# Ups and downs in groups of three or four, with attention scores ahead of ups and attention outputs ahead of downs

## The chip, the cores and the metric

The kernel runs on one core of one Trainium2 chip. The metric is the device time of one execution in microseconds (us); lower is better. The engines of the core work side by side, each through its own list of instructions in order: TensorE (PE: matmuls, PEld: its weight loads), VectorE (DVE), ScalarE (ACT), GpSimd (POOL) and SyncE (SP, which issues most DMAs here). They wait for one another through semaphores.

## The reference

Eight batches of 576 tokens go through eight attention heads, four with a local mask and four with a strided one; the 4608 rows of 512 numbers that come out go through a feed-forward layer with a squared ReLU. All of it is float32.

```python
scores = scale * np.matmul(q, k.transpose(0, 1, 3, 2))
mask_local = (rel >= 0) & (rel < stride)                       # heads 0 to 3
mask_strided = (rel >= 0) & (pos[None, :] % stride == pos[:, None] % stride)  # heads 4 to 7
attn = np.exp(scores - max); attn = attn / (sum + 1e-09)
attn_out = np.matmul(attn, v)
x = attn_out.transpose(0, 2, 1, 3).reshape(4608, 512)
h = np.maximum(x @ w_in, 0.0)                                  # 512 -> 2048
out = h * h @ w_out                                            # 2048 -> 512
```

## The kernel before

**Tiles.** The 4608 rows are 12 chunks (`NCHUNK`) of 384 rows (`TC`). The 2048 columns of `h` are 16 slots (`NFT`) of 128. For each chunk `c` and slot `j` there are two pieces of TensorE work:

- an **up** (`up(c, j)`): 12 matmuls of 128x384 into one of three PSUM banks `h`. Each product is made of three, since every float32 is split in a high part and a low part (`xlh`, `xll` for local heads, `xsh`, `xsl` for strided ones). Then ScalarE does the ReLU (L487), the square (L488) and the rounded copy `gh` (L489), and VectorE the rest `gl = h - gh` (L490).
- a **down** (`down(c, j)`): 9 matmuls of 128x512 (L509), for each of three row tiles `y` the products `gh*w_hi`, `gh*w_lo`, `gl*w_hi` in that order. After slot 15 the three `y` are copied out of PSUM (L513) and written by DMA from SP (L514).

**Attention beside it.** While chunk `c` goes through its ups and downs, the attention of chunk `c + 1` is computed. Its four local heads (`pe_head`, chunks 2 to 11; chunks 0 and 1 go another way) are generators whose steps are drawn by `take`: DMA in; split of q and k (`kx`, `qx`: ACT and POOL); **scores** (4 matmuls, L237) with mask and row minimum on DVE (L241, L229); exponentials on ACT (L246), reciprocal of the sums on DVE (L247, L248) and multiplication by it on ACT (L251; for head 3 on POOL, L254); transposes of the result on DVE (L262) and its split (`px`: L270, L271, L272); **outputs** (4 matmuls, L283), put together by ACT (L286) and DVE (L287, L288) and split into `xlh`, `xll`. The strided heads run without TensorE: POOL multiplies (L426, L448), DVE sums up (L427, L449), in short pieces that `strided` yields and the loop draws at a given pace, for every slot a share.

**Order.** In chunk 0 each slot's up is followed by the down of two slots earlier. From chunk 1 on, slots go in pairs: up, up, then the downs of the two slots before. So a down comes at least two pairs of TensorE work after its up. `gpool` has two buffers for `gh` and two for `gl`: the `gh` of a slot waits for the down of two slots earlier. The table `plan` says between which of these blocks the heads' steps are drawn; scores and outputs stand now ahead of ups, now ahead of downs. `tc.issue_after` pins the order on TensorE. On the other engines the order in which the instructions of all these parts stand comes from the builder's scheduler; it is fixed when the program is built.

Of the kernel before, what the change touches and what calls it, by code (L numbers as in the profile page):

```python
# [18 lines left out]
STR = 32  # L19
# [26 lines left out]
WRATE = 2  # L46

# [39 lines left out]
def attn_moe(ctx: ExitStack, tc, qk_l, v_l, qk_d, v_d, qk_p, v_p, f_s, q_s, k_s, v_s, w_in, w_out, masks, eye, out):  # L87
# [4 lines left out]
    xpool = pool("xpool", 2)  # L92
    gpool = pool("gpool", 2)
    ypool = pool("ypool", 3)
# [4 lines left out]
    ps_y = pool("ps_y", NTT, space=PSUM)  # L99
    ps = pool("ps", 1, space=PSUM)  # L100

    def psum(i, nm):
# [96 lines left out]
    def pe_head(c, h):  # L199
# [60 lines left out]
        for r in range(QC // STR):  # L260
            for k in (r, r + 1):
                nc.vector.transpose(  # L262
                    out=pt[STR * k : STR * (k + 1), :, STR * r : STR * (r + 1)],
                    in_=e.rearrange("p (w k) -> p w k", k=KW)[STR * r : STR * (r + 1), :, STR * k : STR * (k + 1)],
                )
        src = pt.rearrange("p w q -> p (w q)")
        px = lpool.tile([P, 2, TC], F32R, name=f"px{u}", tag="px")

# [26 lines left out]
    def pe_pair(c, pr, local, qk, vr, es, pt, banks, sm, single):  # L295
# [67 lines left out]
        yield  # L363
        p4 = pt.rearrange("p (h w q) -> p h w q", h=2, w=NW)
        for h in range(2):
            t = s_ps[h] if s_ps else banks()

            for w in [*range(NW)] * (2 if c == 0 and local and not pr and h else 1):
                nc.tensor.transpose(t[:kw, w * QC : (w + 1) * QC], e4[h][:, w], ident[:QC, :QC])  # L369
            if c == 0 and not local:  # L370
                nc.vector.tensor_copy(pt[:kw, h * TC : (h + 1) * TC], t[:kw, :TC])
            else:
                last["a"] = nc.scalar.copy(pt[:kw, h * TC : (h + 1) * TC], t[:kw, :TC])
        yield
        x = x_tiles(c)
        if local:
            o = s_ps[0] if s_ps else banks()

            for w in [*range(NW)] * (3 if c == 0 and not pr else 1):
                for h in range(2):  # L380
                    nc.tensor.matmul(o[D * h : D * (h + 1), w * QC : (w + 1) * QC], v4[:kw, h, w], p4[:kw, h, w], start=True, stop=True)  # L381
            outs = [(o[:, :TC], [x["l", s][:, pr, :] for s in "hl"])]
        else:
# [3 lines left out]
            for a in range(2):  # L387
                o = s_ps[a]
                for w in range(NW):
                    for h in range(2):  # L390
                        p0 = r0 + STR * h
                        nc.tensor.matmul(o[p0 : p0 + STR, w * QC : (w + 1) * QC], v4[:kw, h, w, STR * a : STR * (a + 1)], p4[:kw, h, w], start=True, stop=True)
                by_i = lambda t: t[r0 : r0 + D].rearrange("p (s i r) -> p s i r", s=2, r=STR)
# [72 lines left out]
    def up(c, j):  # L466
# [4 lines left out]
        for kt in range(4):  # L471
# [3 lines left out]
            for w, xx in ((wi[p][0], xh), (wi[p][0], xl), (wi[p][1], xh)):  # L475
                done = nc.tensor.matmul(ph[:, :TC], w[:, wsl], xx, start=n == 0, stop=n == 11)  # L476
# [16 lines left out]

    def down(c, j):
        gh, gl = g_tiles.pop((c, j))
        p, o = divmod(j, 2)
# [8 lines left out]
        wsl = slice(o * DM, (o + 1) * DM)  # L505
        for t in range(NTT):
            sl = slice(t * P, (t + 1) * P)
            for k, (g, w) in enumerate(((gh, wo[p][0]), (gh, wo[p][1]), (gl, wo[p][0]))):
                done = nc.tensor.matmul(y_ps[c][t], g[:, sl], w[:, wsl], start=j == 0 and k == 0, stop=j == NFT - 1 and k == 2)  # L509
        if j == NFT - 1:  # L510
            for t in range(NTT):
                y = ypool.tile([P, DM], F32, name=f"ysb{c}_{t}", tag="ysb")
                (nc.scalar.copy if t == 1 else nc.vector.tensor_copy)(y, y_ps[c][t])  # L513
                nc.sync.dma_start(out=out[c * TC + t * P : c * TC + (t + 1) * P, :], in_=y)  # L514
        return done
# [17 lines left out]


    def pair_at(c, pr, local, place, psum_at):
        u = f"{c}_{pr}_{int(local)}"
        buf = lambda pl, nm, n, tag, **kw: pl.tile([P, n], F32, name=f"{nm}{u}", tag=tag, **kw)
        ee = lambda pl, tag: [buf(pl, f"e{h}", 512, tag) for h in range(2)]
        if place == 0:
            b = buf(lraw, "qk", TC + KC, "qk"), buf(lpool, "v", 512, "vx", bufs=1), ee(lpool, "e"), buf(lpool, "pt", 2 * TC, "px")  # L540
        elif place == 1:
            b = buf(lraw, "qk", TC + KC, "qk"), buf(ypool, "v", 512, "ysb"), ee(ypool, "ysb"), buf(lpool, "pt", 2 * TC, "px")
        elif place == 2:
            e = buf(xpool, "e", 2 * TC, "xlh")
            b = buf(xpool, "qk", 2 * TC, "xll"), buf(xpool, "v", 2 * TC, "xsl")[:, :512], [e[:, :TC], e[:, TC:]], buf(lpool, "pt", 2 * KC, "kx", bufs=1)[:, : 2 * TC]
        else:

            t = buf(wpool, "w", 2048, "w7")
            b = buf(xpool, "qk", 2 * TC, "xsh"), buf(spool, "v", 512, "s3", bufs=5), [t[:, :512], t[:, 512:1024]], t[:, 1024 : 1024 + 2 * TC]
        it = iter(range(10))  # L550
# [9 lines left out]
    def local(c):  # L560
# [7 lines left out]
    heads = {}  # L568
    plan = {
        0: ("", "0", "01"),  # L570
        1: ("", "1", "012"),
        2: ("", "0", "123"),
        3: ("", "1", ""),
        4: ("2", "", "23"),
        5: ("3", "", "23"),
        6: ("2", "", "3"),
        7: ("3", "", ""),
    }
# [74 lines left out]

    NS = NCHUNK * NFT
    for s in range(NS + 2):
        c, j = divmod(s, NFT)
        if s < NFT:

            with ExitStack() as seq:
                if s:  # L660
                    seq.enter_context(tc.issue_after(last["up"].ins))
                last["up"] = up(c, j)
            if s >= 2:
                last["pe"] = down(*divmod(s - 2, NFT))

        elif s % 2 == 0:
            before, between, rest = plan[j // 2]
            for part, slots, two in (up, (s, s + 1), before), (down, (s - 2, s - 1), between):
                take(c + 1, two)
                with tc.issue_after(last["pe"].ins):  # L670
                    for i in slots:
                        if 0 <= i < NS:
                            last["mm"] = part(*divmod(i, NFT))
                last["pe"] = last["mm"]
            take(c + 1, rest)
        if s < NFT - 2:

            weights = behind({"a": last["gh"]} | ({"x": last["xs"]} if s > NFT - 4 else {}), ungated)
            for _ in range(WRATE):
                next(weights, "end")  # L680
            weights_end = {e: last[e] for e in "agsv"}
        if s == LATER:
            zbank = (4,)
        if s == NFT - 1:
            with tc.issue_after(weights_end["g"].ins):
                for t in p_t:
                    nc.gpsimd.memset(t, 0.0)
        if j == NFT - 2:
            take(c + 2, "010")
        if c + 1 < NCHUNK and s >= LATER:  # L690
            j0 = LATER if c == 0 else 0
# [16 lines left out]
            if j == NFT - 1:  # L708
                run(lo)
                run(st)  # L710


# [74 lines left out]
```

## Time and profile before

| | |
|---|---|
| device time, median of 3 runs | 880.53 us (880.1 to 881.49) |
| the profiled execution, first to last instruction (span) | 877.8 us, 2.7 us under that median; its own whole time is not listed |
| chunk 6, from its first up to that of chunk 7 (452.14 to 522.21 us) | 70.07 us |
| TensorE busy in the span | 99% |
| VectorE, ScalarE, GpSimd busy | 73%, 65%, 77% |
| granted TensorE clock, mean of the span | 0.999 |

A busy TensorE is not one at its peak: matmuls overlap, and a record's length (334 to 392 ns) is longer than the step from one matmul to the next. The view by time gives the steps. The view of waits names, for each engine, what ended the idle time ahead of an instruction; idle time of an engine that nobody waits for costs nothing.

### The profile page before, as it was taken

What the parts mean: (1) busy time and instruction counts of PE and PEld (TensorE: products, weight loads), DVE (VectorE), ACT (ScalarE), POOL (GpSimd) and SP (SyncE); (2) the same over time, 40 slices, a digit from 0 to 9 for tenths busy, and PEclk for the clock granted to TensorE, in tenths of its full rate; (3) what the DMA queues carried; (4) which work ended last, traced back from release to release, by engine and by line L of the source; (5) the groups of instructions that cost most, each with busy time, mean ns of one, the idle gap of its engine ahead of it and who ended that gap; (6) DMA issues with size and microseconds to landing.
All of it is one profiled execution on the core that took longest, in us unless ns stands there. A gap on an engine that the chain in (4) does not pass through costs nothing.

```text
span 877.8 us, 14934 instructions
## 1 busy us (share of the span) xinstructions
PE 867.9 (99%) x4787; PEld 788.9 (90%) x4787; DVE 640.3 (73%) x1900; ACT 571.4 (65%) x1506; POOL 672.2 (77%) x718
## 2 busy tenths in 40 slices
PE   8999999999999999999999999999999999999997
PEld 7788899999999999999989898989898989999996
DVE  5796587797787887878878779878778787883111
ACT  6998776586576666657756758657666665664332
POOL 3689778877978989888988978996998899782000
PEclk9999999999999999999999999999999999999999
DMA  9963531223123023112102302312031021000000
GB/s 351 363 212 95 178 95 46 85 84 114 32 86 103 27 89 103 44 62 87 58 9 80 116 13 77 100 32 75 31 103 58 29 71 62 7 0 15 23 1 37
DMA packets 26799, 71.42 MB, mean 81 GB/s; under 512 B 2976, under 2 KB 8736, under 8 KB 25184
## 3 DMA queue, kind: packets, MB, share of 16 engines
q1 hardware_dynamic: 26432, 70.14, 24.1%
q8 instruction: 38, 0.62, 0.3%
q14 instruction: 41, 0.34, 0.1%
q10 hardware_dynamic: 288, 0.33, 0.1%
HBM read 61.01 MB, written 9.44 MB: 80 GB/s over the span
## 4 chain that ended last, share of the span: by engine, by line
PE 95%; ACT 2%; POOL 1%; issue 0%; DVE 0%; DVEq 0%; POOLq 0%; ACTq 0%
PE h L476 45%; PE y L509 45%; PE s L237 2%; PE o L283 2%; ACT b L353 1%; PE w_ps L606 1%; PE b L325 1%; POOL w L173 1%; ACT raw L154 0%; ACT z L166 0%; POOL pq L426 0%; ACT w L172 0%; PE b L381 0%; ACT xsh L396 0%; PE b L369 0%
## 5 line engine op out<-in xcount | busy, mean ns | idle before, releaser
L509 PE MATMUL y<-w,gh 128*128 128x512 f32 x1152 | 357.9, 391 | 0.5 <-POOL w L173 0.5
L509 PEld LDWEIGHTS y<-w,gh 128*128 128x128 f32 x1152 | 212.7, 188 | 40.5 <-POOL w L173 0.8
L476 PE MATMUL h<-xlh,w 128*128 128x384 f32 x768 | 229.1, 339 | 1.3 <-ACT xlh L396 0.6
L448 POOL TENSOR_TENSOR pp<-vs,sc 128x448 f32<-128x448 f32 (+10 forms) x192 | 190.0, 1014 | 48.8 <-DVE qs L449 23.0
L476 PE MATMUL h<-xsh,w 128*128 128x384 f32 x768 | 226.4, 335 | 0.3 <-POOL w L173 0.3
L509 PE MATMUL y<-w,gl 128*128 128x512 f32 x576 | 225.2, 392 | 0.0
L426 POOL TENSOR_TENSOR pq<-ks,qs 128x512 f32<-128x512 f32 (+2 forms) x192 | 197.7, 1050 | 18.8 <-DVE sc L427 13.3
L490 DVE TENSOR_TENSOR gl<-h,gh 128x384 fp32r<-128x384 f32 x192 | 105.5, 550 | 80.9 <-ACT gh L489 79.8
L489 ACT CAST gh<-h 128x384 fp32r<-128x384 f32 x192 | 91.8, 478 | 104.3 <-PE y L509 103.3
L487 ACT ACTIVATE h<-h 128x384 f32<-128x384 f32 x176 | 83.1, 472 | 109.8 <-PE h L476 109.3
L427 DVE TENSOR_REDUCE sc<-pq 128x8 f32<-128x512 f32 (+4 forms) x228 | 119.7, 534 | 45.1 <-POOL pq L426 41.9
L476 PEld LDWEIGHTS h<-xlh,w 128*128 128x128 f32 x768 | 141.3, 188 | 4.9 <-ACT w L172 0.9
L476 PEld LDWEIGHTS h<-xsh,w 128*128 128x128 f32 x768 | 141.3, 188 | 1.1 <-POOL w L173 0.6
L476 PE MATMUL h<-xll,w 128*128 128x384 f32 x384 | 129.0, 336 | 0.0
L509 PEld LDWEIGHTS y<-w,gl 128*128 128x128 f32 x576 | 108.1, 188 | 22.9
L476 PE MATMUL h<-xsl,w 128*128 128x384 f32 x384 | 128.4, 334 | 0.0
L449 DVE TENSOR_REDUCE qs<-pp 128x64 f32<-128x448 f32 (+11 forms) x192 | 106.4, 562 | 27.3 <-POOL pp L448 25.5
L488 ACT ACTIVATE h<-h 128x384 f32<-128x384 f32 x176 | 83.3, 473 | 3.6
L262 DVE STREAM_TRANSPOSE p_t<-e 32x128 f32<-32x128 f32 x240 | 72.3, 301 | 11.2 <-ACT e L251 6.6
L476 PEld LDWEIGHTS h<-xll,w 128*128 128x128 f32 x384 | 72.2, 188 | 2.4 <-DVE xll L397 0.3
L476 PEld LDWEIGHTS h<-xsl,w 128*128 128x128 f32 x384 | 72.1, 188 | 0.2
L246 ACT ACTIVATE e<-e,nm 96x128 f32<-96x128 f32 x160 | 62.5, 392 | 10.1 <-DVE nm L229 8.7
(101 smaller groups left out, 1076.7 us busy)
## 6 DMA issues: line engine op xcount, KB each, us to landing
qk<-qk_l SPq DMA_DIRECT2D x24, 400.0 KB, 3.2
y<-ysb SPq DMA_DIRECT2D x36, 256.0 KB, 3.5
raw<-w_in SPq DMA_DIRECT2D x7, 1024.0 KB, 10.9
qk<-qk_l SPq DMA_DIRECT2D x16, 416.0 KB, 3.6
vs<-v_s SPq DMA_DIRECT2D x10, 576.0 KB, 3.9
raw<-w_out SPq DMA_DIRECT2D x5, 1024.0 KB, 12.6
v<-v_l SPq DMA_DIRECT2D x40, 128.0 KB, 2.1
ks<-k_s SPq DMA_DIRECT2D x8, 576.0 KB, 3.8
```

The costliest lines, as they stand in the source:

```text
L246: nc.scalar.activation(e[:QC, cut(w)], e[:QC, cut(w)], AF.Exp, bias=nmax[:QC, w : w + 1], scale=-1.0, accum_out=ssum[:QC, w, :1])
L262: nc.vector.transpose(out=pt[STR * k : STR * (k + 1), :, STR * r : STR * (r + 1)], in_=e.rearrange("p (w k) -> p w k", k=KW)[STR * r : STR ...
L426: nc.gpsimd.tensor_mul(pv, kt[:, a : a + m, :], qt[:, i - i0 : i - i0 + 1, :].broadcast_to([P, m, D]))
L427: nc.vector.tensor_reduce(out=sc[:, i - i0, a : a + m], in_=pv, op=ALU.add, axis=AX.X)
L448: nc.gpsimd.tensor_mul(pv, vt[:, a : a + nd, :n], sc[:, il : il + 1, :n].broadcast_to([P, nd, n]))
L449: nc.vector.tensor_reduce(out=ot[:, il, a : a + nd], in_=pv, op=ALU.add, axis=AX.X)
L476: done = nc.tensor.matmul(ph[:, :TC], w[:, wsl], xx, start=n == 0, stop=n == 11)
L487: nc.scalar.activation(g, g, AF.Relu)
L488: nc.scalar.activation(g, g, AF.Square)
L489: last["gh"] = nc.scalar.copy(gh, g)
L490: nc.vector.tensor_sub(gl, g, f32(gh))
L509: done = nc.tensor.matmul(y_ps[c][t], g[:, sl], w[:, wsl], start=j == 0 and k == 0, stop=j == NFT - 1 and k == 2)
```

## The change

From chunk 1 on the 16 slots of a chunk go in groups of 3, 3, 3, 3 and 4: all ups of the group, then all downs of the same group. The downs of a group no longer lag behind by a pair. A head's scores stand ahead of the ups of one group (heads 0 to 3 in groups 0 to 3), its outputs ahead of the downs of the next. `gpool` gets three sets of one `gh` and one `gl` each, used in turn (in chunk 0 two of them). The third set is at first the transposed probabilities of a pair of local heads (`pt1`), and `px` goes from two buffers to one. In the last group of the last chunk the downs of its last three slots go tile by tile, so that the first two `y` are finished early; the last `y` is copied in two halves, by DVE and ACT, and written by two DMAs from SP and ACT. The strided pieces of a group's slots are drawn partly between ups and downs, partly behind the downs.

```diff
+GROUPS = (3, 3, 3, 3, 4)
...
-    gpool = pool("gpool", 2)
+    gpool = pool("gpool", 1)
...
+    g_pair = lambda i, dtype=F32R: [gpool.tile([P, TC], dtype, name=f"g{i}{k}", tag=f"g{i}{k}") for k in "hl"]
...
-        px = lpool.tile([P, 2, TC], F32R, name=f"px{u}", tag="px")
+        yield
+        px = lpool.tile([P, 2, TC], F32R, name=f"px{u}", tag="px", bufs=1)
...
-        gh = gpool.tile([P, TC], F32R, name=f"gh{c}_{j}", tag="gh")
-        gl = gpool.tile([P, TC], F32R, name=f"gl{c}_{j}", tag="gl")
+        gh, gl = g_pair(j % 2 if c == 0 else (c * NFT + j) % 3)
...
-    def down(c, j):
-        gh, gl = g_tiles.pop((c, j))
+    def down(c, j, tiles=range(NTT)):
+        gh, gl = g_tiles.pop((c, j)) if tiles[-1] == NTT - 1 else g_tiles[c, j]
...
-        for t in range(NTT):
+        for t in tiles:
...
+                if c == NCHUNK - 1 and t == NTT - 1:
+                    half = slice(0, DM // 2), slice(DM // 2, DM)
+                    nc.vector.tensor_copy(y[:, half[0]], y_ps[c][t][:, half[0]])
+                    nc.scalar.copy(y[:, half[1]], y_ps[c][t][:, half[1]])
+                    nc.sync.dma_start(out=rows[:, half[0]], in_=y[:, half[0]])
+                    nc.scalar.dma_start(out=rows[:, half[1]], in_=y[:, half[1]])
...
+    def on_pe(parts):
+        with tc.issue_after(last["pe"].ins):
+            for part, *which in parts:
+                pe = part(*which)
+        last["pe"] = pe
...
-            before, between, rest = plan[j // 2]
-            for part, slots, two in (up, (s, s + 1), before), (down, (s - 2, s - 1), between):
-                take(c + 1, two)
...
+    for c in range(1, NCHUNK):
+        j = 0
+        for g, n in enumerate(GROUPS):
+            slots = range(j, j + n)
+            if g < HL:
+                take(c + 1, (g,))
+            if g:
+                take(c + 1, (g - 1,))
+            on_pe([(up, c, i) for i in slots])
+            if g < HL:
+                take(c + 1, (g,))
+            if g:
+                take(c + 1, (g - 1,))
+            for i in slots[: n // 2]:
+                pace(c, i)
+            if c == NCHUNK - 1 and g == len(GROUPS) - 1:
+                on_pe([(down, c, slots[0])])
+                for t in range(NTT):
+                    on_pe([(down, c, i, (t,)) for i in slots[1:]])
+            else:
+                on_pe([(down, c, i) for i in slots])
+            for i in slots[n // 2 :]:
+                pace(c, i)
+            if g < HL:
+                take(c + 1, (g,))
+                if g < HL - 1:
+                    take(c + 1, (g + 1,))
...
```

Line numbers move by 4 to 13: L487, L488, L489, L490 become L491, L492, L493, L494; L251 becomes L255, L262 L266, L286 L291, L287 L292, L288 L293, L449 L454, L427 L432.

Two places show how the rows stand. **First place:** VectorE in chunk 6, between the `gl` of slot 3 and that of slot 4 (`qs<-pp` are strided sums, `p_t<-e` the transposes of head 1, `e<-o` the outputs of head 0). Before:

```order
L490 TENSOR_TENSOR gl_3_5880<-h_3_5866,gh_3_5879 128x384
L449 TENSOR_REDUCE qs_1_5812<-pp_1_14_0_6298 128x32
L262 STREAM_TRANSPOSE p_t_91<-e_1_5708 32x4x32 x6
L449 TENSOR_REDUCE qs_1_5812<-pp_1_14_32_6392 128x32
L449 TENSOR_REDUCE qs_1_5812<-pp_1_15_0_6395 128x32
L287 TENSOR_TENSOR e_0_5703<-o_0_5930,e_0_5703 64x192
L287 TENSOR_TENSOR e_0_5703<-o_0_6017,e_0_5703 64x192
L449 TENSOR_REDUCE qs_1_5812<-pp_1_15_32_6398 128x32
L288 TENSOR_TENSOR e_0_5703<-o_0_5930,e_0_5703 64x192
L288 TENSOR_TENSOR e_0_5703<-o_0_6017,e_0_5703 64x192
L449 TENSOR_REDUCE qs_1_5812<-pp_1_16_0_6401 128x22
L490 TENSOR_TENSOR gl_4_5984<-h_4_5970,gh_4_5983 128x384
```

Of the change, the same stretch (`g0l`, `g1l` are the `gl` of slots 3 and 4):

```order
L494 TENSOR_TENSOR g0l<-h_3_5941,g0h 128x384
L454 TENSOR_REDUCE qs_1_5825<-pp_1_14_32_6428 128x32
L266 STREAM_TRANSPOSE p_t_91<-e_1_5589 32x4x32 x6
L454 TENSOR_REDUCE qs_1_5825<-pp_1_15_0_6431 128x32
L292 TENSOR_TENSOR e_0_5416<-o_0_5937,e_0_5416 64x192
L292 TENSOR_TENSOR e_0_5416<-o_0_6017,e_0_5416 64x192
L454 TENSOR_REDUCE qs_1_5825<-pp_1_15_32_6434 128x32
L494 TENSOR_TENSOR g1l<-h_4_5960,g1h 128x384
```

Slot 4's `gl` still stands behind the six transposes, a strided sum and the two output rows; two sums and two output rows fewer stand ahead of it. Between the end of slot 4's up and the start of its down lay, on TensorE, three ups, two downs and two outputs; now one up, one down and one outputs lie there.

ScalarE at the same place, before (`n` of the text below is L251, the multiplication by the reciprocal):

```order
L489 CAST gh_3_5879<-h_3_5866 128x384
L251 ACTIVATE e_1_5708<-e_1_5708,rs_1_5886 96x128 x4
L487 ACTIVATE h_4_5970<-h_4_5970 128x384
L488 ACTIVATE h_4_5970<-h_4_5970 128x384
L271 CAST px_1_6052<-p_t_91 128x384
L487 ACTIVATE h_5_5989<-h_5_5989 128x384
```

and of the change:

```order
L491 ACTIVATE h_4_5960<-h_4_5960 128x384
L493 CAST g0h<-h_3_5941 128x384
L255 ACTIVATE e_1_5589<-e_1_5589,rs_1_5923 96x128 x4
L492 ACTIVATE h_4_5960<-h_4_5960 128x384
L491 ACTIVATE h_5_5979<-h_5_5979 128x384
```

The multiplications, and with them the transposes on VectorE, now stand behind the ReLU of slot 4, and so behind the end of its up.

**Second place:** VectorE in chunk 4, around the transposes of head 2 (`sc<-pq` are strided sums), before:

```order
L248 RECIPROCAL rs_2_4456<-rs_2_4456 96x4
L427 TENSOR_REDUCE sc_0_4944<-pq_0_13_0_5084 128x8
L262 STREAM_TRANSPOSE p_t_90<-e_2_4216 32x4x32 x6
L427 TENSOR_REDUCE sc_0_4944<-pq_0_13_8_5087 128x6
L490 TENSOR_TENSOR gl_8_4483<-h_8_4469,gh_8_4482 128x384
```

and of the change:

```order
L252 RECIPROCAL rs_2_4373<-rs_2_4373 96x4
L432 TENSOR_REDUCE sc_0_4957<-pq_0_11_0_5013 128x8
L266 STREAM_TRANSPOSE p_t_90<-e_2_4199 32x4x32 x6
L432 TENSOR_REDUCE sc_0_4957<-pq_0_11_8_5016 128x4
L494 TENSOR_TENSOR g1l<-h_6_4391,g1h 128x384
```

Here the transposes stand ahead of the `gl` of slot 6, the first slot of the third group, whose down is the first of that group.

More of the change, by code (lines that the diff above doesn't have):

```diff
@@ L568, in attn_moe @@
     heads = {}
[L569 to L578, printed above, removed]
     def take(c, which):
@@ L652, in attn_moe, with pace @@
     zbank = (3, 4)
[L654 to L666, printed above, removed]
-            before, between, rest = plan[j // 2]
-            for part, slots, two in (up, (s, s + 1), before), (down, (s - 2, s - 1), between):
-                take(c + 1, two)
[L670 to L690, printed above, removed]
+    def pace(c, j):
+        nonlocal lo, st, dl, ds, cost
+        if c + 1 < NCHUNK and (c or j >= LATER):
             j0 = LATER if c == 0 else 0
@@ L710, in attn_moe @@
                 run(st)
+    lo = st = dl = ds = cost = None
+    for j in range(NFT):
+        with ExitStack() as seq:
+            if j:
+                seq.enter_context(tc.issue_after(last["up"].ins))
+            last["up"] = up(0, j)
+        if j >= 2:
+            last["pe"] = down(0, j - 2)
+        if j < NFT - 2:
+            weights = behind({"a": last["gh"]} | ({"x": last["xs"]} if j > NFT - 4 else {}), ungated)
+            for _ in range(WRATE):
+                next(weights, "end")
+            weights_end = {e: last[e] for e in "agsv"}
+        if j == LATER:
+            zbank = (4,)
+        if j == NFT - 1:
+            with tc.issue_after(weights_end["g"].ins):
+                for t in p_t:
+                    nc.gpsimd.memset(t, 0.0)
+            for i in (NFT - 2, NFT - 1):
+                on_pe([(down, 0, i)])
+        if j == NFT - 2:
+            take(2, "010")
+        pace(0, j)
+    for c in range(1, NCHUNK):
[17 more added lines that the diff above has]
+                    on_pe([(down, c, i, (t,)) for i in slots[1:]])
+            else:
+                on_pe([(down, c, i) for i in slots])
[5 more added lines that the diff above has]
+                    take(c + 1, (g + 1,))
+                if g < 2:
+                    take(c + 1, (g + 2,))
+                elif g == 2:
+                    take(c + 2, (0,))
+                else:
+                    take(c + 2, (1,))
+                    take(c + 2, (0,))
+            j += n
 _NAMES = ["qk_l", "v_l", "qk_d", "v_d", "qk_p", "v_p", "f_s", "q_s", "k_s", "v_s", "w_in", "w_out", "masks", "eye"]
```

27 lines of the change are left out of this document (15 added, 12 removed).

## The prediction

> **What bounds the kernel now.** First the page: span, share of each engine, clock.
>
> ```profile
> span 877.8 us, 14934 instructions
> PE 867.9 (99%) x4787; PEld 788.9 (90%) x4787; DVE 640.3 (73%) x1900; ACT 571.4 (65%) x1506; POOL 672.2 (77%) x718
> PEclk9999999999999999999999999999999999999999
> ```
>
> TensorE fills the span at full clock. The view by stretches says the same of one whole chunk, the sixth:
>
> ```profile
> 452.14:522.21 70.07, 70.07 (x370) 64.08 (x369) 56.13 (x159) 45.86 (x126) 64.50 (x66) 1.00 0.21 66
> ```
>
> In 70.07 us TensorE never idles; VectorE works 56.1 of them (80%), GpSimd 64.5 (92%). So only two things change the time: how TensorE's own rows follow each other, and whether anything makes it wait. The view by time shows the steps in that chunk:
>
> ```profile
> 465.11 0.64 PE L237 MATMUL s<-kx,qx 128*96 128x256 f32 x4
> 465.59 0.62 PE L509 MATMUL y<-w,gh 128*128 128x512 f32 x2
> ...
> 469.71 0.33 PE L476 MATMUL h<-xlh,w 128*128 128x384 f32 x1
> ...
> 471.82 0.33 PE L476 MATMUL h<-xlh,w 128*128 128x384 f32 x1
> ...
> 473.90 0.58 PE L283 MATMUL o<-px,vx 128*128 128x192 f32 x4
> 474.33 0.64 PE L509 MATMUL y<-w,gh 128*128 128x512 f32 x2
> 474.81 0.39 PE L509 MATMUL y<-w,gl 128*128 128x512 f32 x1
> ...
> 476.39 0.62 PE L509 MATMUL y<-w,gh 128*128 128x512 f32 x2
> ...
> 478.43 0.33 PE L476 MATMUL h<-xlh,w 128*128 128x384 f32 x1
> ```
>
> Scores take 0.48 us, outputs 0.43. An up behind a switch takes 2.11 (469.71 to 471.82), the one behind an up 2.08; a down 2.06 behind a switch (474.33 to 476.39), then 2.04. A down's third matmul, its first with `gl`, starts 0.48 into it.
>
> **Fewer switches: minus 3.3 us.** Sixteen ups at 2.08, sixteen downs at 2.04 and four scores and outputs make 33.28 + 32.64 + 1.92 + 1.72 = 69.56 us; the chunk takes 70.07, so its 16 switches cost 0.51, 0.03 each. Ten are left: 0.2 saved; that scores and outputs now stand only where their neighbours are the cheaper ones I estimate at another 0.1 from the spread of those steps (2.08 to 2.11, 2.04 to 2.06). 11 chunks by 0.3 are 3.3. The most that could go is all of it, 5.6; the least nothing.
>
> **The end: minus 1 us.**
>
> ```profile
> 872.69 1.29 DVE L513 COPY ysb<-y 128x512 f32<-128x512 f32 x2 [2.74 <-PE y L509]
> 873.41 1.31 SPq L514 DMA_DIRECT2D y<-ysb  x3
> y<-ysb SPq DMA_DIRECT2D x3, 256.0 KB, 2.3
> ```
>
> Two copies and three DMA issues follow each other behind the last matmul; then a write lands in 2.3 us. Now one copy of half the width and one issue on each of two queues are left: between 0.3 (half a copy) and 1.4 (two issues of 0.44 and half a copy besides); I take 1.0.
>
> **The wait that goes.**
>
> ```profile
> ACT gh L489 <- PE y L509: 103.3, 108, 1.6
> DVE sc L427 <- POOL pq L426: 41.9, 66, 2.2
> DVE qs L449 <- POOL pp L448: 25.5, 45, 1.5
> ```
>
> ScalarE waited 103 us for downs to free `gh`. With three sets that is gone but for a group's fourth slot. TensorE never waited for it, so alone it brings nothing.
>
> **The wait that comes.** Before, `gh` of a slot could be written from the end of the down two slots earlier, and was needed one down and two ups later, 6.2 us. Now let 0 be the end of a group's third up. The ups end at -4.16, -2.08 and 0; outputs follow, then the downs at 0.43, 2.49 and 4.55, and their `gl` are needed at 0.91, 2.97 and 5.03 (0.43 earlier in the first group, which has no outputs). Between an up and its `gl` stand ScalarE's and VectorE's other rows, in a fixed order. What these take, in the same chunk:
>
> ```profile
> 465.44 0.47 ACT L487 ACTIVATE h<-h 128x384 f32<-128x384 f32 x1
> 465.85 0.52 ACT L220 CAST kx<-qk 128x416 fp32r<-128x416 f32 x1
> ...
> 467.10 0.38 ACT L246 ACTIVATE e<-e,nm 96x128 f32<-96x128 f32 x1
> ...
> 469.06 0.45 ACT L489 CAST gh<-h 128x384 fp32r<-128x384 f32 x1
> ...
> 470.12 1.28 ACT L251 ACTIVATE e<-e,rs 96x128 f32<-96x128 f32 x4
> 472.02 0.47 ACT L487 ACTIVATE h<-h 128x384 f32<-128x384 f32 x1 [0.62 <-PE h L476]
> 472.52 0.47 ACT L488 ACTIVATE h<-h 128x384 f32<-128x384 f32 x1
> ```
>
> ```profile
> 466.02 0.74 DVE L241 TENSOR_TENSOR e<-s,mask_sb 96x256 f32<-96x256 f32 x2
> ...
> 471.84 1.87 DVE L262 STREAM_TRANSPOSE p_t<-e 32x128 f32<-32x128 f32 x6
> 473.74 1.25 DVE L449 TENSOR_REDUCE qs<-pp 128x32 f32<-128x480 f32 x2
> 475.01 0.61 DVE L287 TENSOR_TENSOR e<-o,e 64x192 f32<-64x192 f32 x2
> 475.75 0.69 DVE L449 TENSOR_REDUCE qs<-pp 128x32 f32<-128x512 f32 x1
> 476.36 0.60 DVE L288 TENSOR_TENSOR e<-o,e 64x192 f32<-64x192 f32 x2
> ...
> 477.33 0.54 DVE L490 TENSOR_TENSOR gl<-h,gh 128x384 fp32r<-128x384 f32 x1
> ```
>
> A ReLU starts 0.20 behind its up (471.82, 472.02). A ScalarE row that waits for nothing holds the queue 0.41, a ReLU whose square follows 0.50.
>
> *First place (slots 3 to 5 of chunk 6).* ScalarE: ReLU of slot 4 at -2.08 + 0.20 = -1.88, `gh` of slot 3 at -1.47, the four multiplications from -1.06 to 0.22. VectorE is through with slot 3's `gl` and a sum by 0.1; then transposes take 1.90 (471.84 to 473.74), a sum 0.63, two output rows 0.61, a sum 0.61, so `gl` of slot 4 runs from 3.99 to 4.53. Needed at 2.97: **TensorE waits 1.6 us**. The trace of before took 4.52 from the first transpose to 476.36 over the same rows and one sum more, so the chain isn't an artefact of adding up.
>
> *Second place (slots 6 to 8 of chunk 4).* Scores end at -6.3; the first exponential comes 1.08 behind the first VectorE row (466.02 to 467.10), about -5.2; exponentials and the copy among them take 1.96 (467.10 to 469.06), ReLU and square 0.91, the multiplications 1.28: -1.05. Transposes 1.90 and a small sum, 0.4, bring `gl` of slot 6 to 1.25 to 1.79. Needed at 0.91: **0.9 us**.
>
> By the order, the first three groups of the ten chunks that carry heads (30 groups) divide so: seven have the first shape (chunks 2, 4, 6, 8, 9; both groups of 6 and 8), at 1.2 to 2.2 each by the rows between transposes and `gl`, 10.7 together; seven have the second, 0.85 each, 6.0; in chunk 5 the exponentials stand behind the second slot's `gh`, and the third slot's `gl` comes 1.7 late; fifteen wait 0 to 0.9, together 4. Groups 3 and 4 and the last chunk have room: in group 3 GpSimd does the multiplication and only the third `gl` stands behind the transposes; in group 4 the waiting `gh` of the fourth slot is needed 6.6 us in. That is 22.4. VectorE's waits for GpSimd (67 us in all, above) come on top where a sum stands ahead of `gl`: I add 2, 0.1 for each group that waits. **Plus 24.4.** If every chain were 0.6 shorter, some 12 are left; 0.6 longer everywhere, near 40. Behind a late `gl` are queued on TensorE the rest of that down, the next scores and ups; a stall is never made up, since TensorE has no idle time.
>
> At the turn from chunk 0 to 1 scores still end with GpSimd's split of `qx`, whichever block stands ahead of it: nothing.
>
> **The sum.** Made against the span: 877.8 - 3.3 - 1.0 + 24.4 = 897.9; with the 2.7 us by which the median lies above that span, 900.6. I forecast **900**.
>
> **Rivals.**
>
> *VectorE keeps up.* If every first `gl` is through by 0.9 and every second by 3.0, only the gains remain: 880.5 - 4.3 = **876**, faster. It decides at 1.6 us in the first place and 0.9 in the second. For it: ScalarE is freed of 103 us of blocking, so multiplications could come earlier. Against: at the first place their start hangs on the end of an up, and transposes alone take 1.90.
>
> *Short stalls.* Half the chains 0.8 shorter than I make them: about 8 us of stalls, **884**.
>
> *GpSimd and VectorE fall behind together.* GpSimd is 92% busy in the chunk and may run only two products ahead; a VectorE queue held by a late `gh` holds GpSimd too. If each of 50 groups lost 0.4 more, 20 us: **920**; from 908 on I count it here.
>
> *The clock falls.* A matmul unit that stops two or three times a chunk might lose its clock.
>
> ```profile
> 26.00:45.00 19.00, 17.45 (x99) 14.95 (x96) 13.19 (x26) 18.93 (x33) 13.91 (x15) 1.00 0.83 329
> ```
>
> Early on TensorE idles 1.55 of 19 us, and the granted clock stays 1.00, which speaks against it. If one group a chunk (12.9 us of rows) ran at half clock, ten chunks would add 129 us: **1029**. The Trainium skill's page "TensorE: Matmul & The Clock Gate", section "A second HAM failure mode: psum-queue depth-cycling", says that short idle times between groups of matmuls can make the clock go back and forth, which speaks for this rival; by it the sum would be that 1029, by the row above 900. That row disagrees with the page so far.
>
> **How the numbers follow.** Forecast case (stalls of 12 to 32 us, 888 to 908): 0.68. VectorE keeps up: 0.14. Short stalls (879 to 888): 0.10, half of which I count within 0.2% of before. Falling behind (908 to 925): 0.06. Clock: 0.02. 0.2% (1.8 us) is about what a measurement of this kernel can tell from no change. So faster 0.14, same 0.05, slower 0.81. The range leaves out the fast rival and the far tail: 880 to 914.
>
> **What would show it.** In the changed profile: idle time of TensorE ahead of downs released by VectorE's `gl`, one to three times a chunk, 0.5 to 2 us, in groups 0 to 2 and hardly in group 4 or the last chunk; chunks of 72 to 73 us while heads run and under 70 in the last; ScalarE's wait of `gh` for downs nearly gone. Wrong would be: no such idle time and chunks of 69.7 (then the chain on VectorE is shorter than I read it), stalls released by ScalarE's `gh` or by GpSimd's `qx`, or a clock under 1.

## The result and the profile after

The changed kernel takes 893.13 us (median of 4 runs, 892.32 to 893.99); the kernel before, run beside it, 880.71 (880.1 to 881.49). The ratio is 1.0145, 95% interval 1.0133 to 1.0156: slower by 12.4 us. The forecast was 900, the range 880 to 914. One execution of all the runs reported here, of the kernel `before_with_new_end`, was granted a clock of 0.557 and took 1439.49 us; it is left out of that run's ratio.

The page of the changed kernel, with the same three lines as before:

```profile
span 890.5 us, 14769 instructions
PE 872.5 (98%) x4787; PEld 785.0 (88%) x4787; DVE 637.6 (72%) x1900; ACT 565.3 (63%) x1507; POOL 673.1 (76%) x718
PEclk9999999999999999999999999999999999999999
```

The span grew by 12.7 us. TensorE runs as many matmuls as before (4787), no other engine is busy for more than 0.9 us longer, and the clock stayed full. So TensorE waits. For what, the view of waits says for TensorE and ScalarE (engine, line, releaser; us in all, times, longest):

```profile
PE y L513 <- DVE g1l L494: 2.9, 7, 0.8
PE y L513 <- DVE g0l L494: 2.0, 5, 0.7
...
PE y L513 <- DVE g2l L494: 1.1, 2, 0.8
...
PE o L288 <- DVE px L277: 0.9, 1, 0.9
PE y L513 <- ACT g1h L493: 0.8, 1, 0.8
...
ACT kx L224 <- PE s L241: 64.5, 25, 4.3
```

ScalarE's wait of `gh` for downs (103.3 us before) is gone but for 3.8 us. ScalarE now waits for scores (`kx`, 64.5 us; 1.6 before) and, at the end of a chunk, for its last downs (`ysb`, 37.9; 4.9 before); its wait for ups fell from 109.3 to 82.0. Such waits cost nothing by themselves. What is new is that TensorE waits for `gl`, once for `px` (not foreseen) and for some `gh`. The listed idle time is less than what is lost: the records of matmuls overlap, so a short wait shows no idle time at all. A sound sum is the whole stretch from the first up of chunk 1 to the start of the last matmul. The view by stretches (length, then busy time of PE, PEld, DVE, ACT, POOL, clock, DMA share, GB/s) has for before this stretch, and within it chunk 1:

```profile
99.78:872.71 772.93, 772.35 (x4050) 705.18 (x4049) 565.93 (x1668) 484.79 (x1327) 600.37 (x634) 1.00 0.19 60
...
99.78:171.89 72.11, 71.53 (x386) 64.64 (x384) 54.43 (x179) 47.23 (x132) 57.93 (x73) 1.00 0.31 96
```

for the changed kernel:

```profile
106.96:886.14 779.18, 770.83 (x4014) 696.89 (x4012) 563.09 (x1661) 477.06 (x1324) 596.35 (x629) 1.00 0.18 58
```

and for an experiment described below, in which the same order of ups and downs runs without any wait (`trans_mult_behind`), the stretch and chunk 6:

```profile
107.49:870.75 763.26, 763.26 (x4013) 699.31 (x4012) 560.66 (x1661) 484.30 (x1324) 596.41 (x629) 1.00 0.19 59
...
456.51:526.32 69.81, 69.81 (x370) 63.87 (x369) 56.34 (x164) 46.06 (x128) 62.41 (x64) 1.00 0.20 66
```

From these the 12.7 us divide so:

- **Waits: +15.9** (779.18 - 763.26). By the steps from one matmul to the next, 21 waits of 0.2 to 1.1 us make 11.8 of them: 17 for `gl` (9.1), three for `gh` (1.6) and the one for `px` (1.1). The rest are shorter ones and the delay of a follower that the last section shows.
- **Switches: -3.1.** Before, the stretch holds two downs of chunk 0 and one scores block more than now (2 x 2.04 + 0.48 = 4.56), and 2.04 us of leftovers of chunk 0 in chunk 1 (72.11 against the 70.07 of a later chunk). 772.93 - 4.56 - 2.04 = 766.33, against 763.26.
- **The entry of chunk 1: +0.6.** Chunk 1 begins 7.18 us later (106.96 - 99.78); 4.56 and 2.04 of them are the moved pieces. One trace does not settle so small a number: with the same order of ups and downs the first up of chunk 1 starts anywhere from 106.48 to 108.36 in the other kernels' traces, and in the old order's trace of `before_with_new_end_2` the leftovers are 2.9 us.
- **The end: -0.7.** From the start of the last matmul to the end of the span it is 890.5 - 886.14 = 4.4, before 877.8 - 872.71 = 5.1.

Now the first place of the prediction, chunk 6, slots 3 to 5. The view by time, TensorE first (start, length; outputs begin at 483.35, the prediction's 0):

```profile
483.35 0.59 PE L288 MATMUL o<-px,vx 128*128 128x192 f32 x4
...
485.84 1.55 PE L513 MATMUL y<-w,g1h 128*128 128x512 f32 x6
487.76 0.96 PE L513 MATMUL y<-w,g1l 128*128 128x512 f32 x3 [0.38 <-DVE g1l L494]
...
482.37 0.56 DVE L494 TENSOR_TENSOR g0l<-h,g0h 128x384 fp32r<-128x384 f32 x1 [0.93 <-ACT g0h L493]
482.85 0.64 DVE L454 TENSOR_REDUCE qs<-pp 128x32 f32<-128x480 f32 x1
483.53 1.88 DVE L266 STREAM_TRANSPOSE p_t<-e 32x128 f32<-32x128 f32 x6
485.45 0.69 DVE L454 TENSOR_REDUCE qs<-pp 128x32 f32<-128x512 f32 x1
486.05 0.60 DVE L292 TENSOR_TENSOR e<-o,e 64x192 f32<-64x192 f32 x2
486.58 0.67 DVE L454 TENSOR_REDUCE qs<-pp 128x32 f32<-128x512 f32 x1
487.17 0.54 DVE L494 TENSOR_TENSOR g1l<-h,g1h 128x384 fp32r<-128x384 f32 x1
...
482.22 1.28 ACT L255 ACTIVATE e<-e,rs 96x128 f32<-96x128 f32 x4
```

The chain is the forecast one, to 0.2 us: multiplications on ScalarE, transposes and sums on VectorE, and `g1l` at 3.82 to 4.36 (forecast 3.99 to 4.53). But the down of slot 4 does not take its `gl` as third matmul. The rows of TensorE show six products with `g1h` in a row, then three with `g1l`, so `gl` is needed at the seventh. The seventh would have started 1.36 us into the down (six steps of 0.227), at 3.85 (2.49 + 1.36), and starts at 4.41: a wait of 0.56. The scheduler has put 140 of the chunks' downs in this order; before, nearly all took `gh`, `gh`, `gl` for each row tile, as the code lists them.

### The profile page after: what moved, and what is told of

The parts are those of the page before. It is cut to its first block, busy times and chain, and to the rows that moved or that the text cites. A ratio compares the mean times of both kernels' runs of the same rounds, so it can differ in the third digit from the quotient of the medians.

```text
span 890.5 us, 14769 instructions
## 1 busy us (share of the span) xinstructions
PE 872.5 (98%) x4787; PEld 785.0 (88%) x4787; DVE 637.6 (72%) x1900; ACT 565.3 (63%) x1507; POOL 673.1 (76%) x718
## 4 chain that ended last, share of the span: by engine, by line
PE 74%; DVE 9%; POOL 7%; ACT 7%; issue 2%; POOLq 0%; DVEq 0%; ACTq 0%
PE y L513 36%; PE h L481 35%; DVE p_t L266 3%; POOL pq L431 2%; POOL pp L453 2%; PE s L241 2%; POOL w L177 1%; DVE sc L432 1%; PE o L288 1%; DVE qs L454 1%; ACT e L250 1%; POOL qx L227 1%; ACT h L491 1%; ACT b L358 1%; ACT e L255 1%
## 5 line engine op out<-in xcount | busy, mean ns | idle before, releaser
L432 DVE TENSOR_REDUCE sc<-pq 128x8 f32<-128x512 f32 (+4 forms) x228 | 119.5, 534 | 52.8 <-POOL pq L431 50.5
L491 ACT ACTIVATE h<-h 128x384 f32<-128x384 f32 x176 | 82.4, 468 | 90.7 <-PE h L481 82.0
L454 DVE TENSOR_REDUCE qs<-pp 128x64 f32<-128x448 f32 (+11 forms) x192 | 106.5, 562 | 29.8 <-POOL pp L453 28.4
L513 PE MATMUL y<-w,g1h 128*128 128x512 f32 x402 | 110.1, 393 | 1.8 <-POOL w L177 1.0
L513 PE MATMUL y<-w,g0h 128*128 128x512 f32 x396 | 108.7, 392 | 0.2 <-ACT g0h L493 0.2
L513 PE MATMUL y<-w,g2h 128*128 128x512 f32 x354 | 95.0, 392 | 0.1
L513 PEld LDWEIGHTS y<-w,g1h 128*128 128x128 f32 x402 | 74.0, 188 | 17.7 <-POOL w L177 1.8
L513 PEld LDWEIGHTS y<-w,g0h 128*128 128x128 f32 x396 | 73.1, 188 | 14.9 <-ACT g0h L493 1.1
L492 ACT ACTIVATE h<-h 128x384 f32<-128x384 f32 x176 | 83.7, 476 | 2.9
L513 PEld LDWEIGHTS y<-w,g2h 128*128 128x128 f32 x354 | 65.3, 188 | 13.4 <-ACT g2h L493 0.8
L266 DVE STREAM_TRANSPOSE p_t<-e 32x128 f32<-32x128 f32 x240 | 72.2, 301 | 6.0 <-ACT e L255 2.6
```

The source lines that it names most:

```text
L266: nc.vector.transpose(out=pt[STR * k : STR * (k + 1), :, STR * r : STR * (r + 1)], in_=e.rearrange("p (w k) -> p w k", k=KW)[STR * r : STR ...
L432: nc.vector.tensor_reduce(out=sc[:, i - i0, a : a + m], in_=pv, op=ALU.add, axis=AX.X)
L454: nc.vector.tensor_reduce(out=ot[:, il, a : a + nd], in_=pv, op=ALU.add, axis=AX.X)
L491: nc.scalar.activation(g, g, AF.Relu)
L492: nc.scalar.activation(g, g, AF.Square)
```

## The experiments

The theory: TensorE waits because the downs follow their own ups, and between an up and its `gh` and `gl` the heads' rows (multiplications on ScalarE, transposes and sums on VectorE) stand in the same queues. Rivals: the smaller buffers make the wait; VectorE and GpSimd have too much to do; the order of the downs' products. An ordering edge on one engine can move a row behind another one without taking any wait away, so most of the edits are such edges.

**Transposes behind the last `gl`** (`transposes_behind`).

```diff
+        last["gl"] = nc.vector.tensor_sub(gl, g, f32(gh))
...
+        with tc.issue_after(last["gl"].ins):
         for r in range(QC // STR):
             for k in (r, r + 1):
                 nc.vector.transpose(
...
```

> The changed kernel, with one edit: the six transposes of a head stand on VectorE behind the last gl of the group in whose downs they are drawn, instead of wherever the scheduler put them. Theory (gl is late because it queues behind the transposes): a gl of the first place comes 1.9 us earlier, so nearly all waits released by gl go, some 10 to 12 of the 14.5 us; what is left are waits for gh (0.3 to 0.9 us, a handful) and the 0.5 us at the entry of chunk 1. 880 to 883 us. Rival 'the smaller buffers' (px with one buffer, three sets of gh and gl): nothing moves, 893. Rival 'GpSimd and VectorE have not enough time between them': the waits move to outputs and scores, 889 or more.

Measured: 883.01 us, ratio to before 1.0029 (1.0018 to 1.0041). The stretch from chunk 1 on is 769.63 us, so 6.4 us of waits are left of 15.9. The lines view of this kernel (times, then busy and mean ns, then idle before it and its releaser):

```profile
L514 PE MATMUL y<-w,g0h 128*128 128x512 f32 x396 | 108.7, 392 | 1.0 <-ACT g0h L494 1.0
L514 PE MATMUL y<-w,g2h 128*128 128x512 f32 x354 | 94.9, 392 | 0.6 <-ACT g2h L494 0.6
L514 PE MATMUL y<-w,g1l 128*128 128x512 f32 x201 | 63.1, 392 | 0.4 <-DVE g1l L495 0.3
```

Idle time released by `gl` falls from 6.0 us to under 0.5; what remains is mostly released by `gh`, on ScalarE. The buffers are the same as in the changed kernel, so they alone are not the cause.

**Multiplications too** (`trans_mult_behind`).

```diff
+            with tc.issue_after(last["gh"].ins):
             for w in range(NW):
                 nc.scalar.mul(e[:QC, cut(w)], e[:QC, cut(w)], rs[:QC, w : w + 1])
```

> As the run with the transposes behind the last gl, and besides the four multiplications of a head by 1/sum (ScalarE) stand behind the last gh of the group. Theory: the waits for gh go as well, so what is left of the change is 0.5 us at the entry of chunk 1, -1.6 from fewer switches and -0.7 at the end: 879 us, a little under the kernel before. Rival 'the smaller buffers': 893. Rival 'a new wait': the outputs then wait for px of the head before, which starts 2 us later: up to 0.5 us in each of 40 groups, so 885 to 900.

Measured: 876.92 us, ratio 0.9956 (0.9941 to 0.997). All waits behind the entry are gone; TensorE is busy in the whole stretch (763.26 of 763.26, above). This kernel is faster than both. The same rows of VectorE in chunk 6, where outputs now begin at 475.73:

```profile
474.83 0.56 DVE L496 TENSOR_TENSOR g0l<-h,g0h 128x384 fp32r<-128x384 f32 x1 [0.78 <-ACT g0h L495]
475.36 0.69 DVE L456 TENSOR_REDUCE qs<-pp 128x32 f32<-128x512 f32 x1
475.96 0.55 DVE L496 TENSOR_TENSOR g1l<-h,g1h 128x384 fp32r<-128x384 f32 x1
...
479.59 1.88 DVE L268 STREAM_TRANSPOSE p_t<-e 32x128 f32<-32x128 f32 x6
```

`g1l` now ends at 0.78 on the prediction's scale, 3.6 us earlier, and the transposes lie beside the downs, where nobody waits.

**Multiplications alone** (`mult_behind`): the second edge without the first.

> The changed kernel with the multiplications alone behind the last gh of the group; the transposes stand where the scheduler puts them. Since a head's transposes need its products, they follow behind the last gl by themselves in 30 of the 40 groups, and stay ahead of slot 11's gl for the heads whose product GpSimd forms. Theory: nearly all waits go, 877 to 880. Rival 'only the transposes' place counts, and the multiplications' does not' can't be told apart by the time, but by the rows: a multiplication ahead of gh delays gl by 1.28 us on ScalarE whatever VectorE does.

Measured: 876.92 us, ratio 0.9959 (0.9944 to 0.9975); the stretch is 763.15 us. A head's transposes need its products, so one edge on ScalarE pulls most transposes behind as well. It is the smaller of the two edits that remove the whole loss.

**`gl` products early** (`gl_right_behind`): in each down from chunk 1 on, the matmuls are tied in the order of the code.

```diff
+                with ExitStack() as st:
+                    if c and done is not None:
+                        st.enter_context(tc.issue_after(done.ins))
                     done = nc.tensor.matmul(y_ps[c][t], g[:, sl], w[:, wsl], start=j == 0 and k == 0, stop=j == NFT - 1 and k == 2)
```

> The changed kernel, with one edit on TensorE: in each down from chunk 1 on the three products of a row tile follow each other (gh, gh, gl for each tile), as the code lists them; the scheduler had put all three gl products of a down behind its six gh products in 140 of its downs. So a down needs its gl 0.89 us earlier. Theory (the wait is gl's lateness against that deadline): every wait for a gl of a first or second slot grows by up to 0.89 us: 14 to 20 of them, and some that were hidden appear; +8 to +16 us, 900 to 909. Rival 'TensorE waits for something that the products' order doesn't touch': 893. Rival 'the switches between weights of gh and gl cost': a change of the steps themselves, seen in chunk 11, which has no waits.

Measured: 922.84 us, ratio 1.0481 (1.0465 to 1.0497); the direction as expected, the size two to four times as large. Three rows of its lines view and the stretch:

```profile
L517 PE MATMUL y<-w,g1l 128*128 128x512 f32 x201 | 80.6, 401 | 10.6 <-DVE g1l L494 10.5
L517 PE MATMUL y<-w,g0l 128*128 128x512 f32 x198 | 78.4, 397 | 6.8 <-DVE g0l L494 6.8
L517 PE MATMUL y<-w,g2l 128*128 128x512 f32 x177 | 72.0, 407 | 11.4 <-DVE g2l L494 11.0
...
106.48:916.48 810.00, 779.69 (x4013) 698.03 (x4012) 563.81 (x1661) 474.90 (x1324) 597.37 (x629) 1.00 0.18 56
```

TensorE loses 46.7 us (810.00 - 763.26), nearly all in waits for `gl`; up to 3.4 us of it are the clock's, which was at 0.50 for two stretches of 3.41 us (last section). So the order of products that the scheduler chose saves some 30 us in this kernel. The scheduler also set other engines' rows anew for this kernel, so the 30 us are not the edge's alone.

**Both edges, and `gl` products early** (`behind_gl_right_behind`).

> Transposes and multiplications behind the last gl and gh, and in each down the gl product of a tile right behind its two gh products (the order that cost 30 us in the changed kernel). Theory (the late deadline for gl only mattered because heads' rows stood ahead of gl): a first gl then comes about 2.1 us behind the end of its up, at -2.0, and is needed at 0.9, so there is room of 2.9: no waits, 877. Rival 'the order hhl itself is slower (weights of gl between those of gh)': chunks longer than 69.8 without waits, 885 or more. Rival 'a first gl waits for GpSimd's sums anyway': waits of 0.5 us at some 10 places, 882.

Measured: 877.65 us, ratio 0.997 (0.9959 to 0.998); the stretch is 764.06 us, 0.8 of waits. With the heads' rows out of the way the order of the products is worth 0.8 us, not 30: it isn't slow by itself.

**The buffers alone** (`three_sets_old_order`): order and end of the kernel before, with three sets of `gh` and `gl` and one `px`.

> The kernel before, with the buffers of the change alone: three sets of gh and gl, px with one buffer, the pair's transposed probabilities in the third set; order and end as before. Theory (buffers alone bring and cost nothing, since TensorE waited for none): 880.7, within 1 us; ScalarE's wait of gh for downs shrinks from 103 us. Rival 'px with one buffer costs': outputs wait for px, 885 or more. Rival 'the freed ScalarE lets all run earlier': under 879.

Measured: 880.49 us, ratio 0.9999 (0.999 to 1.0008): nothing, as expected.

**Transposes twice** (`transposes_twice`, and with both edges `behind_transposes_twice`).

```diff
-            for k in (r, r + 1):
+            for k in (r, r + 1) * 2:
```

> The changed kernel with each transpose of a head done twice (the second writes the same numbers): 1.9 us more on VectorE for each of 40 heads, wherever the scheduler puts them. Theory: the waits of TensorE grow, by up to 1.9 us at the 20 places where transposes stand ahead of the gl that is waited for: +15 to +35 us, 908 to 928. Rival 'VectorE's amount of work sets the time': the same here, but then also in the next run.

> Transposes and multiplications behind the last gl and gh, each transpose done twice. Theory (place, not amount): VectorE has 76 us more to do and TensorE doesn't wait for it, 876 to 879. Rival 'VectorE's amount of work': as much more as in the run before, 890 or more.

Measured: 976.73 us, ratio 1.1093 (1.106 to 1.1126), and 915.6 us, ratio 1.0407 (1.0389 to 1.0425). Both missed. The stretches are these, the first kernel's ahead of the second's:

```profile
107.11:967.28 860.17, 792.36 (x4013) 703.29 (x4012) 640.27 (x1901) 479.83 (x1324) 597.37 (x629) 0.98 0.17 53
```

```profile
107.53:908.84 801.31, 776.07 (x4013) 699.88 (x4012) 630.40 (x1901) 476.89 (x1324) 596.42 (x629) 1.00 0.18 57
```

40 heads by 1.88 us are 75 us of additional work on VectorE. In the changed kernel TensorE pays 81 for them (860.17 - 779.18); up to 14 of these are the clock's, which was at 0.50 for 27.3 us of the stretch (last section). Behind the last `gl` it pays 38 (801.31 - 763.26), at full clock. So the place decides about 59 us at equal work, the clock's part among them, but the room behind the downs isn't unlimited, as I had expected it to be: roughly half of 1.88 us for each head. How the second kernel comes to wait, the view by time shows in one group:

```profile
149.59 0.64 DVE L268 STREAM_TRANSPOSE p_t<-e 32x128 f32<-32x128 f32 x2
...
150.26 0.51 ACT L278 CAST px<-p_t 128x384 fp32r<-128x384 f32 x1 [2.98 <-DVE p_t L268]
...
153.71 0.47 ACT L493 ACTIVATE h<-h 128x384 f32<-128x384 f32 x1
...
154.97 0.50 ACT L495 CAST g1h<-h 128x384 fp32r<-128x384 f32 x1
...
155.52 1.67 PE L515 MATMUL y<-w,g1h 128*128 128x512 f32 x6 [1.10 <-ACT g1h L495]
```

ScalarE sits 2.98 us at `px`, waiting for transposes that end late; exponentials and the next group's first ReLU are queued behind it, and so the first `gh` comes 1.1 us late. The wait has moved into the next group.

**The end alone** (`before_with_new_end`, `before_with_new_end_2`: the kernel before with the last copy halved over two engines and two queues; the second is the same kernel again).

> The kernel before with the end of the change alone: the last y is copied in two halves by VectorE and ScalarE and written by two queues. (The downs' order by tiles in the last group is not taken over.) By the prediction's term -1.0 us (-0.3 to -1.4); by the end of the changed kernel's trace -0.7, since the ScalarE half began only when the VectorE half was through. Theory: 879.8 to 880.1, that is -0.4 to -0.7. Rival 'the end of the change is worth nothing, its shorter end comes from the order of the downs by tiles': 880.5.

> Once more the kernel before with the copy of the last y in two halves and two queues alone, to see its trace: by the changed kernel's trace the stretch from the start of the last matmul to the end shrinks from 5.08 us to 4.4 or 4.5; by the prediction's term to 4.1. If it stays at 5.1, the end's gain comes from the downs by tiles, which this kernel lacks. The time, which an earlier run left within 0.1% of before: 880.

Measured: 880.06 us, ratio 1.0 (0.9991 to 1.0009), and 880.47, ratio 1.0001 (0.9992 to 1.0009). From the last matmul's start (874.02) to the end (879.2) it is 5.2 us, not less than before. Its end by time:

```profile
873.99 0.69 DVE L521 COPY ysb<-y 128x512 f32<-128x512 f32 x1 [2.74 <-PE y L509]
...
874.60 0.41 DVE L516 COPY ysb<-y 128x256 f32<-128x256 f32 x1
...
875.05 0.37 ACT L517 COPY ysb<-y 128x256 f32<-128x256 f32 x1 [0.25 <-DVE ysb L516]
875.45 0.35 ACTq L519 DMA_DIRECT2D y<-ysb  x1
875.62 0.40 SPq L518 DMA_DIRECT2D y<-ysb  x1
```

VectorE's half waits for its copy of the first `y`, and ScalarE's half for VectorE's. The edit alone brings nothing; by elimination, what the changed kernel gains at its end needs the downs by tiles, which finish the first two `y` early. The downs by tiles alone were not run.

**Two halves in two tiles, and the entry** (`behind_two_tiles`, `behind_two_tiles_entry`), both on top of the two edges.

```diff
+                    y2 = lpool.tile([P, 512], F32, name=f"ysb{c}_{t}b", tag="e")
-                    nc.scalar.copy(y[:, half[1]], y_ps[c][t][:, half[1]])
+                    nc.scalar.copy(y2[:, : DM // 2], y_ps[c][t][:, half[1]])
...
-            if g < HL:
+            if g < HL and (c > 1 or g):
                 take(c + 1, (g,))
...
             on_pe([(up, c, i) for i in slots])
             if g < HL:
-                take(c + 1, (g,))
+                take(c + 1, (g,) if c > 1 or g else (g, g))
```

> The kernel with transposes and multiplications behind gl and gh (876.9 us), with the ScalarE half of the last y copied into a tile of its own. Theory (the two halves ran one after the other because both write one tile): they run side by side, the ScalarE half begins 0.4 us earlier, and the second write is issued 0.4 us earlier; the end gains 0.2 to 0.4 us: 876.5 to 876.7. Rival 'both read one PSUM bank and so follow each other anyway': 876.9, with the same wait of ScalarE's copy.

> As the run with two tiles, and in the first group of chunk 1 alone the scores stand behind the ups, as in the kernel before, since GpSimd's qx isn't ready when chunk 1 begins (0.68 us of waiting at the scores, and small ones ahead of them). Theory (the entry of chunk 1 costs 0.5 us because of the place of these scores): the wait goes or shrinks, 876.0 to 876.3. Rival 'whatever stands there waits for GpSimd' (the prediction's: nothing): no change, 876.6. Rival 'the first group now has its exponentials behind its downs' and a later wait in chunk 1 takes the gain': 876.6 or more.

Measured: 877.52 us, ratio 0.997 (0.9961 to 0.9979), and 876.4, ratio 0.9959 (0.9945 to 0.9973). The first is no gain on the 876.92 without it: ScalarE's copy still waits for VectorE's, though it writes another tile:

```profile
872.05 0.42 DVE L522 COPY ysb<-y 128x256 f32<-128x256 f32 x1 [3.39 <-PE y L515]
...
872.56 0.37 ACT L524 COPY ysb_2b<-y 128x256 f32<-128x256 f32 x1 [1.96 <-DVE ysb L522]
```

So it isn't the shared target; what both halves still share is the PSUM bank that they read. Whether that makes them follow each other was not tried. With the scores of the entry behind the ups, their wait is gone from the trace: from the first up of chunk 0 to that of chunk 2 it takes 150.46 us (26.76 to 177.22), against 151.19 with two tiles alone (27.00 to 178.19). In both, the last down of chunk 0, just ahead, waits 1.0 us for its weights `w`; the kernel with the two edges alone, whose trace lacks that wait, takes 150.33 (26.98 to 177.31) with its scores still ahead. So a gain is not settled by the traces either. Against the 876.92 of the kernel with the two edges alone the time does not settle whether that is a gain, since the three intervals overlap.

## Why the prediction was right, and where it wasn't

Verdict, range and mechanism were right; the forecast was 7 us too high, and it came that near probably in part by luck, since two errors in its largest term ran against each other. Step by step:

- **Fewer switches, -3.3:** -3.1. Right, also in its size for one chunk: 70.07 before, 69.81 without waits, 0.26 where 0.3 was forecast.
- **The end, -1.0:** -0.7, within its bounds. The reason given, half a copy and two queues, is not enough: alone they bring nothing.
- **The wait that goes, 0:** 0, shown by the buffers alone (ratio 0.9999).
- **The turn from chunk 0 to 1, 0:** +0.6. In the changed kernel the scores of chunk 1 stand ahead of its first up and wait for `qx`, and the up behind them:

```profile
105.35 1.01 POOL L227 TENSOR_TENSOR qx<-qk,qx 64x384 fp32r<-64x384 f32 x1
...
106.41 0.71 PE L241 MATMUL s<-kx,qx 128*96 128x256 f32 x4 [0.52 <-POOL qx L227]
...
106.96 0.34 PE L481 MATMUL h<-xlh,w 128*128 128x384 f32 x1
```

The prediction had said that the scores wait there in any order. True, but it had not asked who is queued behind them. With the scores behind the ups this wait is not there (the last experiment). The last down of chunk 0, now also ahead of that up, waits 0.57 us for its weights in this trace; that is hidden, since `qx` comes later still.

- **The wait that comes, +24.4:** +15.9. This is the term that was mis-sized. The arrival of `gl` was right to 0.2 us at the first place; the deadline, "a down's third matmul, its first with `gl`, starts 0.48 into it", was read from the kernel before and is wrong for the changed one, where most downs take `gl` at the seventh matmul, 1.36 us in. At the first place that makes 0.56 of the forecast 1.6. Chunks 1 to 10 take 69.7 to 72.2 us, where 72 to 73 were forecast for those with heads. Three of the 21 waits were for `gh`, which the prediction had named as a sign of being wrong, but they are 1.6 us of 11.8. The order of the changed kernel's rows on TensorE was there to be read; I had read VectorE's and ScalarE's only.
- **The arrivals** erred the other way, at some places at least. With the deadline that I had assumed, the kernel with early `gl` products loses 46.7 us, not 24.4 (with the reservations above, that other rows moved there too and that the clock has a part). The second place, in the changed kernel's trace, shows such an error (outputs begin at 354.87, the prediction's 0):

```profile
353.76 0.69 DVE L432 TENSOR_REDUCE sc<-pq 128x8 f32<-128x512 f32 x1 [1.42 <-POOL pq L431]
354.37 1.87 DVE L266 STREAM_TRANSPOSE p_t<-e 32x128 f32<-32x128 f32 x6
...
357.21 0.96 PE L513 MATMUL y<-w,g1l 128*128 128x512 f32 x3 [0.37 <-DVE g1l L494]
```

A strided sum that waited 1.42 us for GpSimd stands ahead of the transposes. They begin at -0.50, where -1.05 was forecast, and `gl` ends at 2.29, not at 1.79. Here too it is needed at the seventh matmul, due at 1.78, which starts at 2.34: 0.56 us of waiting for a forecast 0.9. So an arrival 0.5 too late and a deadline 0.88 too late partly cancelled. Whether my fifteen "others" at 4 us together were too low as well was not counted.
- **Rival "VectorE keeps up", 876:** not this kernel. But its price is that of the kernel with the heads' rows behind `gh` and `gl`, 876.9: the gains of the change are real, and the order of ScalarE's and VectorE's rows lost them.
- **Rival "GpSimd and VectorE fall behind together":** no. The same amount of work runs without waits once the heads' rows stand behind. With 75 us more on VectorE TensorE waits again even so, by the chain through `px` shown above; whether GpSimd has a part in that was not tried.
- **Rival "the clock falls":** not in this kernel. The mean is 0.999 with waits at 21 places, the longest 1.1 us. The rule of the Trainium skill's page "TensorE: Matmul & The Clock Gate", section "A second HAM failure mode: psum-queue depth-cycling", did not show in the changed kernel. Two experiments whose waits are longer do lose the clock for short stretches (last section).

## What to carry to other kernels

When work is regrouped so that a consumer follows its producer directly, look at what a scheduler puts between them in the in-order queues of the other engines; an ordering edge that moves unhurried rows behind the urgent one can be worth more than the regrouping itself. Read arrival and deadline of an operand both from the changed program: a scheduler that moves the producer's rows moves the consumer's too. Before costing rows that are moved "behind" at nothing, look for the next row that waits for them in an in-order queue, since its wait is passed on to all that stands behind it.

## What the runs showed of the hardware

A matmul that had to wait delays its follower as well. In the kernel with early `gl` products the row behind a wait starts 0.34 us after it, where 0.23 is the step:

```profile
505.09 0.50 PE L517 MATMUL y<-w,g1l 128*128 128x512 f32 x1
505.43 0.63 PE L517 MATMUL y<-w,g1h 128*128 128x512 f32 x2
```

So such a wait costs about 0.11 us more than it lasts, and this one of 0.17 us shows no idle time in the records at all. In the changed kernel the same 0.11 follows each of the 20 waits that stand ahead of a down's matmul.

With longer waits the granted clock falls to half for a short time. In `transposes_twice`, where a chunk takes about 80 us, chunk 6 reads 0.96; the second line is a stretch within it:

```profile
499.00:579.00 80.00, 74.23 (x369) 65.60 (x368) 62.13 (x182) 44.92 (x127) 60.74 (x62) 0.96 0.18 57
528.23:531.64 3.41, 3.41 (x12) 2.67 (x11) 1.27 (x3) 0.09 (x1) 3.27 (x4) 0.50 0.03 5
```

So 0.96 is a mean: full clock, and two stretches of 3.41 us at 0.50 (the other from 545.29). By the clock records of the traces this kernel has seven such stretches, six of 3.41 us and one of 6.83, 27.3 us in all; the kernel with early `gl` products has two of 3.41 us (from 130.65 and 192.09). Each begins within a wait of TensorE that shows 1.6 to 3.4 us of idle time, or at most 1.4 us behind it. Other waits as long (2.5 us, ended at 369.46 in `transposes_twice`) are followed by none. Between the first up of chunk 1 and the last matmul, the kernel before, the changed kernel and those with the heads' rows moved behind have no such stretch. Half the clock is what the rival had assumed, so what keeps it away from the changed kernel seems to be that its waits are short. That the waits bring the fall was not tried by itself.
